# A recurrence with two MLPs behind it on one Trainium2 core: solve products added in place, gate and value as whole groups of eight matmuls, and a planner with numbered passes

## The chip, the cores and the metric

The kernel runs on one core of a Trainium2 chip. The metric is the time of one execution on the device in microseconds; the median of three runs is quoted, and one further execution was profiled.

## The reference, cut to what matters

```python
# batch 4, heads 8, 768 steps, head dimension 40
for t in range(S):                                   # attention-like recurrence
    y[:, :, t] = einsum('bhd,bhde->bhe', rt, state)
    Sa = einsum('bhde,bhe->bhd', state, at)
    state = state * wt[:, :, None, :] - einsum('bhd,bhe->bhde', Sa, bt) \
            + einsum('bhd,bhe->bhde', vt, kt)
x = y.transpose(0, 2, 1, 3).reshape(3072, 320)
h = x @ w_in                                         # 320 -> 2048
x = where(h >= 1, h, where(h <= -1, 0, (h + 1)**2 / 4)) @ w_out
g, val = x @ w_gate, x @ w_val                       # 320 -> 1536 each
out = (g / (1 + exp(-g)) * val) @ w_out2
```

All values are float32. The kernel keeps precision by splitting numbers into two float16 parts (high and low) and adding the products of the parts.

## The kernel before, in words

**Units.** The 768 steps are cut into 12 chunks of 64 steps (`c`); in each chunk there are four units, one for each batch (`j`), so 48 units `n = 4c + j`. Two units of a chunk share several loads and are called a pair (24 pairs, key `("mp", n // 2)`).

**The recurrence.** `p_tasks` prepares a unit's factors, `inv_tasks` inverts a chunk's triangular systems on VectorE (62 dependent small operations, lines L944 and L949, on the array `M`, 128 partitions by 16 by 32) and stores the result to DRAM (`tsd`, L969). `m_tasks` then does a unit's serial part. Its matmuls are, in order: `mm_x` (L1061), the solve product `mm_sa` for the first half of 32 steps (L1071, 8 matmuls, one for each head), `mm_c` (L1077), `mm_sa` for the second half, `mm_q` (L1138), `mm_y` (L1159). Between them ScalarE, VectorE and GpSimd split results into float16 parts (`xhi`, `xlo`, `xdup`, `shi`, `slo`). The stationary operand of `mm_sa` is a slice of the tile `tt`, which holds the inverse of both units of a pair; there is one `tt` buffer, so a pair's two loads (L1032: 64 partitions, L1036: 32 partitions) are issued after the last `mm_sa` of the pair before. `mm_sa` wrote its 32 rows of result to rows 64 to 127 of the PSUM tile `px`, from where `shi` and `slo` read them.

**The MLPs.** For a chunk of 256 tokens (all four batches), `in1` handles 256 hidden columns at a time: 16 matmuls of 128x256 (L1204, two groups of eight), then two ScalarE, one VectorE, one ScalarE and one GpSimd operation, then `outp` (L1293, 12 matmuls of 128x320, in two groups of six). There are 8 such pieces in a chunk. `in2` handles the gate and the value of 256 columns of the second MLP, 6 pieces in a chunk, each with its two PSUM tiles `ph`. The contraction over 320 needs, with the float16 parts, seven products over 128 rows and one over 64 rows. `in2_mm` does the seven (`full`, L1225) for gate and value, and the remaining 64-row products of gate and value in `half` (L1233): the gate's sit in rows 0 to 63 of the array, the value's in rows 64 to 127. Only when `half` is done may the gate's activation (L1276, ScalarE) and then the product with the value (L1279, VectorE) start.

**The order of the work.** All operations are entered as tasks with an engine, a cost, a priority and buffers. The class `Plan` simulates the engines (`forward`), then backward (`backward`) to get better priorities, repeats this, and emits the instructions of each engine in the order of a plan. So each engine's queue is fixed at build time, and TensorE waits in order for whatever stands next. A DMA's landing is assumed at `dma + 1.05`.

Of the kernel before, what the change touches and what calls it, by code (L numbers as in the profile page):

```python
# [15 lines left out]
class Plan:  # L16
# [28 lines left out]
    def task(self, eng, cost, emit, r=(), w=(), use=(), p=0.0, more=0.0, dma=0.0, slow=1.3, lk=False):  # L45
# [3 lines left out]
        for name, key in use:  # L49
# [3 lines left out]
            dma=dma, slow=slow, lk=lk or eng == "Pool", b=self.bias))  # L53
# [11 lines left out]
    def forward(self, prio):  # L65
# [59 lines left out]
        while done < len(ts):  # L125
            started = True
            while started:
                started = False
                for eng in self.ENGINES[:5]:
# [7 lines left out]
                    while any(heaps):  # L137
# [178 lines left out]
    def run(self):  # L316
# [3 lines left out]
        prio, best = [t["p"] + b for t, b in zip(self.tasks, bias)], None  # L320
        for _ in range(self.rounds):
            plan = self.forward(prio)
            if plan is None:
                break
            if best is None or plan[0] < best[0]:
                best = plan
            back = self.backward([-s - c for s, c in zip(plan[1], cost)])
            if back is None:
                break
            prio = [plan[0] - s - c + b for s, c, b in zip(back, cost, bias)]  # L330
# [8 lines left out]
def tile_recurrence__then__gated_mlps(  # L339
# [97 lines left out]
    sbt("tt", [128, 2, 2, H, HC], F16, 1)  # L437
# [102 lines left out]
    def TR(emit, dma, **kw):  # L540
        T("SP", 1.45, emit, dma=dma, **kw)
# [34 lines left out]
    def setup():  # L576
# [29 lines left out]
    def wpiece(names, key, src, n, m, dst_hi, dst_lo, scale, p, fit, r=(), also=None):  # L606
# [68 lines left out]
    def w_in_piece(name, src, dst, i, low, scale):  # L675
        if low:
            cs = slice(256 * i, 256 * i + 512)
            return ([(name, i), (name, i + 1)], (name, i, 2), src[1][i // 2].bitcast(I32), 64,
                    512, dst[0:64, 2, cs], dst[0:64, 2, cs] if name == "wv" else dst[64:128, 2, cs], scale)
# [234 lines left out]
    def inv_tasks(c, p):  # L914
# [38 lines left out]
        for i0 in range(0, 2 * HC - 2, span):  # L953
            part = [divmod(i, 2) for i in range(i0, min(i0 + span, 2 * HC - 2))]

            def steps(part=part):
# [4 lines left out]
              r=[(key, "j", i0)], w=[(key, "j", min(i0 + span, 2 * HC - 2))], use=ub + pm, p=p)  # L961
        T("ACT", c_s(512), lambda: s_.activation(
            out=T16()[:, 0], in_=M(), func=AF.Copy, scale=2.0**8),
          r=[(key, "j", 2 * HC - 2)], w=[(key, "h")], use=ub + pm, p=p)
        T("DVE", c_v(512), lambda: split(T16()[:, 1], M(), 2.0**8, T16()[:, 0]),
# [12 lines left out]
    def split_x(name, key, rows, src, scale, r, w, use, p, pool=False):  # L978
# [9 lines left out]
        def lo():  # L988
            t = x_tile(name, key)
            split(t[rows, 384:704], src(), scale, t[rows, 0:HD], e_)  # L990
            if name == "g":
                e_.tensor_copy(out=t[rows, 704:768], in_=t[rows, 640:704])
# [481 lines left out]
```

## Time and profile before

| | |
|---|---|
| median of three runs | 1107.91 us (1104.25 to 1110.54) |
| profiled execution | 1116.03 us, span 1113.9 us |
| busy TensorE / weight loads / VectorE / ScalarE / GpSimd | 900.9 / 712.6 / 772.2 / 720.0 / 714.1 us |
| granted TensorE clock, mean | 0.972 of full speed |

Busy time is the union of an engine's instructions. TensorE's matmuls are pipelined, so the distance from one matmul's start to the next tells more than the length that the profile shows of each. A share of the whole span hides that the first 400 us and the rest have different limits.

### The profile page before, as it was taken

Reading aid. Unit: us, or ns where it says so; the run is one execution under the profiler, and the core shown is the slowest. Engines: PE = TensorE matmul, PEld = TensorE weight load, DVE = VectorE, ACT = ScalarE, POOL = GpSimd, SP = SyncE. Lnnn points to the kernel's source line nnn. Section 1 sums busy time; section 2 is a strip of 40 time slices with the busy share of each in tenths; the row PEclk is TensorE's granted clock in tenths of the full one; section 3 lists DMA queues with packets and bytes.
Section 4 is the critical chain, followed back from the end, with each engine's and each line's share of the span. In section 5 each row is a group of like instructions: output and inputs, shape, how many; then the busy total and the mean of one; then the engine's idle time right before and its main releaser. Section 6 shows DMA issues by size and latency. Waiting matters only on the chain.

```text
span 1113.9 us, 28813 instructions
## 1 busy us (share of the span) xinstructions
PE 900.9 (81%) x10944; PEld 712.6 (64%) x10944; DVE 772.2 (69%) x1874; ACT 720.0 (65%) x1339; POOL 714.1 (64%) x980
## 2 busy tenths in 40 slices
PE   0321336757876999999999999999998999999998
PEld 0321225535654777877877787777786787787776
DVE  8688897997699577785876958768478477441210
ACT  1785576768776867768767777677686674644422
POOL 4588687756677778677785877758777464432222
PEclk9999999859898999999999999999999999999999
DMA  6976688688798689496794878857884444210000
GB/s 217 193 198 157 194 187 188 175 178 195 128 212 177 140 144 162 92 172 131 152 162 96 156 146 162 140 115 150 129 154 107 93 96 65 47 41 20 15 1 24
DMA packets 386195, 147.94 MB, mean 133 GB/s; under 512 B 344536, under 2 KB 362776, under 8 KB 386056
## 3 DMA queue, kind: packets, MB, share of 16 engines
q1 hardware_dynamic: 357735, 131.79, 57.4%
q10 hardware_dynamic: 28321, 14.31, 6.5%
q8 instruction: 85, 1.39, 0.6%
q14 instruction: 54, 0.44, 0.1%
HBM read 78.25 MB, written 21.52 MB: 90 GB/s over the span
## 4 chain that ended last, share of the span: by engine, by line
PE 34%; DVE 11%; DMA 7%; ACT 6%; issue 3%; POOL 1%; SPq 1%; POOLq 0%; ACTq 0%; DVEq 0%
PE po L1293 11%; PE ph L1225 9%; PE ph L1204 7%; DVE pg L949 2%; DVE ub L944 2%; DMA mx<-x 1%; PE pg L1159 1%; DMA vsT<-vss 1%; DMA tt<-tsd 1%; DVE vss L562 1%; PE ph L1233 1%; PE px L1071 1%; ACT ss L1168 1%; DMA ub<-lsd 1%; DVE mx L1279 1%
## 5 line engine op out<-in xcount | busy, mean ns | idle before, releaser
L1293 PE MATMUL po<-wo,mx 128*128 128x320 f16 x2016 | 320.2, 303 | 4.7 <-POOL mx L560 2.0
L560 POOL TENSOR_TENSOR mx<-mx 128x512 f16<-128x512 f32 x168 | 195.0, 1163 | 159.2 <-ACT mx L1250 146.2
L1293 PEld LDWEIGHTS <-mx 128*128 128x128 f16 x2016 | 187.9, 99 | 82.7 <-issue 14.7
L1204 PE MATMUL ph<-mx,w 128*128 128x256 f16 x1536 | 191.8, 278 | 12.8 <-DMA mx<-x 8.6
L1204 PEld LDWEIGHTS <-w 128*128 128x128 f16 x1536 | 149.6, 100 | 38.0 <-issue 9.7
L1225 PE MATMUL ph<-x2t,wg 128*128 128x256 f16 x1008 | 135.8, 275 | 7.0 <-ACT mx L1276 4.5
L1225 PE MATMUL ph<-x2t,wv 128*128 128x256 f16 x1008 | 135.0, 275 | 3.7 <-DVE mx L1279 1.7
L1250 ACT CAST mx<-mx 128x512 f16<-128x512 f32 x168 | 102.9, 615 | 42.0 <-DVE mx L1266 16.7
L1266 DVE SCALAR_TENSOR_TENSOR mx<-ph,mx 128x512 f32<-128x512 f32 x96 | 66.1, 689 | 77.4 <-ACT mx L1263 76.8
L1225 PEld LDWEIGHTS <-wg 128*128 128x128 f16 x1008 | 96.1, 98 | 23.1 <-issue 4.5
L1225 PEld LDWEIGHTS <-wv 128*128 128x128 f16 x1008 | 97.6, 98 | 17.8 <-issue 2.2
L1279 DVE SCALAR_TENSOR_TENSOR mx<-ph,mx 128x512 f32<-128x512 f32 x72 | 49.5, 687 | 83.7 <-ACT mx L1276 83.0
L944 DVE SCALAR_TENSOR_TENSOR ub<-ub,pg 128x126 f32<-128x126 f32 (+22 forms) x372 | 92.1, 248 | 21.0 <-DMA ub<-lsd 12.4
L949 DVE TENSOR_TENSOR pg<-pg,ub 128x126 f32<-128x126 f32 (+22 forms) x372 | 95.8, 257 | 8.2
L1276 ACT ACTIVATE mx<-ph 128x512 f32<-128x512 f32 x72 | 42.9, 596 | 78.0 <-PE ph L1233 69.9
L566 POOL TENSOR_TENSOR ldp<-ldp 64x320 f32<-64x320 f32 (+1 forms) x90 | 77.3, 869 | 5.1 <-DMA ldp<-was 1.1
L1262 ACT ACTIVATE mx<-ph 128x512 f32<-128x512 f32 x96 | 57.1, 594 | 25.0 <-PE ph L1204 21.6
L1102 ACT ACTIVATE vss<-px 32x640 f16<-32x640 f32 x90 | 62.0, 695 | 16.6 <-PE px L1071 14.1
L1093 POOL COPY xs<-xs 32x320 f16<-32x320 f16 x96 | 42.8, 449 | 31.1 <-ACT xs L1088 25.2
L1263 ACT ACTIVATE mx<-mx 128x512 f32<-128x512 f32 x96 | 60.5, 630 | 3.1
L884 DVE TENSOR_TENSOR pg<-pg,mask 64x512 f32<-64x512 f32 x48 | 33.1, 689 | 37.3 <-PE pg L881 19.4
L562 DVE SCALAR_TENSOR_TENSOR vss<-px,vss 32x320 f16<-32x320 f32 x90 | 44.3, 493 | 19.4 <-ACT vss L1102 16.6
(220 smaller groups left out, 1779.7 us busy)
## 6 DMA issues: line engine op xcount, KB each, us to landing
ub<-lsd SPq DMA_DIRECT2D x24, 256.0 KB
ldp<-in_kb_dram SPq DMA_DIRECT2D x18, 320.0 KB
ldv<-in_v_dram SPq DMA_DIRECT2D x18, 320.0 KB
wo<-in_wo_dram SPq DMA_DIRECT2D x15, 320.0 KB
ldp<-in_ar_dram SPq DMA_DIRECT2D x14, 320.0 KB
out_dram<-mx SPq DMA_DIRECT2D x23, 160.0 KB
ldp<-wks SPq DMA_DIRECT2D x20, 160.0 KB
wo<-in_w1a_dram SPq DMA_DIRECT2D x6, 512.0 KB
```

Source lines behind the costliest of these rows:

```text
L560: e.tensor_tensor(out=out, in0=x, in1=hi, op=ALU.subtract)
L566: e.tensor_tensor(out=out, in0=x, in1=y, op=ALU.mult)
L944: v_.scalar_tensor_tensor(out=t, in0=L()[:, j, j + 1:].unsqueeze(1).to_broadcast([128, nm, ni]), scalar=-(2.0**-10), in1=m[:, 0:nm, j:j + ...
L949: v_.tensor_tensor(out=m[:, 0:nm, j + 1:], in0=m[:, 0:nm, j + 1:], in1=t, op=ALU.add)
L1102: s_.activation(out=hi2(G("vss", key)[z]), in_=two(hd(G("px", key))[z]), func=AF.Copy, scale=2.0**-8)
L1204: t_.matmul(out=ps, lhsT=wts[:, wi, fs], rhs=xT[:, xi, :], start=(i == 0), stop=(i == len(plan) - 1))
L1225: t_.matmul(out=dst(a, f), lhsT=wts[:, wi, fs], rhs=G(*xk)[:, xi, :], start=(n == 0 and f == 0), stop=False)
L1250: T("ACT", c_s(512) - 0.04, lambda: s_.copy(out=G("g", key)[:, 0], in_=u2(key)), r=[(key, "u")], w=[(key, "gh")], use=U + GG, p=p)
L1263: s_.activation(out=u2(key), in_=u2(key), func=AF.Square, scale=2.0**3)
L1266: T("DVE", c_v(512, True), lambda: v_.scalar_tensor_tensor(out=u2(key), in0=ps2(key), scalar=2.0**8, in1=u2(key), op0=ALU.max, op1=ALU.min ...
L1279: T("DVE", c_v(512, True), lambda: v_.scalar_tensor_tensor(out=u2(key), in0=ps2(vk), scalar=2.0**-3, in1=u2(key), op0=ALU.mult, op1=ALU.mult),
L1293: t_.matmul(out=ps, lhsT=g[:, x, f, 128 * tt:128 * tt + 128], rhs=wo[:, 2 * i + f, y, :], start=(i == 0 and f == 0 and m == 0), stop=(i == ...
```

## The change

Four things are done. **(1)** `mm_sa` multiplies by a window of 128 columns of `tt` and adds into the rows of `px` that already hold its input (`start=False`), instead of writing 32 rows elsewhere. For this the inverse has its unit diagonal removed (`strict`, two small VectorE memsets a chunk) and its sign turned, `tt` gets a 64-column grid in which 32 columns are data and 32 are zero (one memset at the start), and its loads write runs of 32 numbers. `shi` and `slo` read the other rows of `px`. **(2)** `in2_mm` is gone: gate and value are each done as `in_mm` does it for the first MLP, two groups of eight matmuls over all 128 rows (the low part of the last 64 rows is padded with zeros, the extra ScalarE copy `also` of the value's weights is dropped), and the activation waits for the gate alone. **(3)** `outp` takes its first and last matmul by a count. **(4)** The planner makes 3 passes, keeps the priorities of the last pass that worked, adds offsets by kind, stage and step before and after the passes, and assumes landings at `dma + 1.705`; some lead times change.

```diff
-        self.bias = 0.0
-        self.lim, self.rounds, self.loose = 1.438, 14, ()
+        self.bias, self.unit, self.nudge, self.last = 0.0, ["z", 0, 0], ({}, {}), ({}, {})
+        self.lim, self.rounds, self.loose = 1.438, 3, ()
...
+    def offset(self, tables, t):
+        return tables[0].get(t["unit"][:2], 0.0) + tables[1].get(t["unit"][::2], 0.0)
...
-                            end = dma + 1.05
+                            end = dma + 1.705
...
+        best = self.forward([x + self.offset(self.last, t) for x, t in zip(good, self.tasks)])
...
-    sbt("tt", [128, 2, 2, H, HC], F16, 1)
+    tts = sbt("tt", [128, 8 * H * HC + HC], F16, 1)
...
+        v_.memset(tts[0], 0.0)
...
-        if also is not None:
-            T("ACT", c_s(m), lambda: s_.activation(
-                out=also, in_=u3(), func=AF.Copy, scale=scale), r=[(key, 3)], w=names, use=ux, p=p)
...
+        def strict():
+            for g in range(2):
+                v_.memset(G("pg", key)[64 * g:64 * g + 64, g:g + 15 * (HC + 2) + 1:HC + 2], 0.0)
+
+        T("DVE", 0.17, strict, r=[(key, "j", 2 * HC - 2)], w=[(key, "m")], use=ub + pm, p=p)
...
+            def tiles(a, b):
+                return G("tt", mp)[a:b, 0:8 * H * HC].rearrange("p (f b x) -> p f b x", f=2, x=C)[:, :, :, 0:HC]
+
             DMA(lambda e: e.dma_start(
-                out=G("tt", mp)[0:64].rearrange("p f j h t -> p f (j h t)"),
-                in_=td.rearrange("l s f b t -> (l s) f (b t)")),
+                out=tiles(0, 64), in_=td.rearrange("l s f b t -> (l s) f b t")),
                 r=[("tsd", c)], w=[(mp, "tt")], use=TT, p=p - 3, dma=0.5)
             DMA(lambda e: e.dma_start(
-                out=G("tt", mp)[64:96].rearrange("p f j h t -> p f (j h t)"),
-                in_=td[0].rearrange("s f b t -> s f (b t)")),
+                out=tiles(64, 96), in_=td[0]),
                 r=[("tsd", c)], w=[(mp, "tt")], use=TT, p=p - 3, dma=0.25, cost=0.68)
...
         def mm_sa(hf):
-            sa, tt, xs = hd(G("px", key)), G("tt", mp)[0:96, hf, j % 2], G("xs", (key, hf))[0:96]
-            z = 64 + 32 * hf
+            sa, tt, xs = hd(G("px", key)), G("tt", mp)[0:96], G("xs", (key, hf))[0:96]
             for h in range(H):
-                t_.matmul(out=sa[z:z + 32, h], lhsT=tt[:, h], rhs=xs[:, h])
+                o = C * (2 * H * hf + H * (j % 2) + h) - HC * hf
+                t_.matmul(out=sa[:, h], lhsT=tt[:, o:o + 128], rhs=xs[:, h], start=False, stop=(h == H - 1),
+                          skip_group_check=True)
...
-    def in2_mm(key, vk, i, xk, p):
...
-        in2_mm(key, vk, i, ("x2t", c), p)
+        in_mm(key, wg, "wg", ("x2t", c), i, p, [("x2t", c)], (key, "h"))
+        in_mm(vk, wv, "wv", ("x2t", c), i, p, [("x2t", c)], (vk, "h"))
...
-          r=[(key, "t")], w=[(key, "u")], use=U + [("ph", vk)], p=p)
+          r=[(key, "t"), (vk, "h")], w=[(key, "u")], use=U + [("ph", vk)], p=p)
...
+    by_chunk = by({
+        "a": {1: 3.58, 3: 1.46, 6: 0.68, 10: -1.14},
...
```

**Order, first place: gate and value on TensorE.** The rows are one of the last pieces of the second MLP, before the change; `ph_131` and `ph_132` are the gate's and the value's PSUM tiles, and only the first rows of each run of equal kind are shown.

```order
L1225 LDWEIGHTS wg
L1225 MATMUL ph_131<-x2t_123,wg 128x256
...
L1225 LDWEIGHTS wv
L1225 MATMUL ph_132<-x2t_123,wv 128x256
...
L1293 MATMUL po_133<-wo_67,mx 128x320
...
L1233 LDWEIGHTS wg
L1233 MATMUL ph_131<-x2t_123,wg 128x256
L1233 LDWEIGHTS wv
L1233 MATMUL ph_132<-x2t_123,wv 128x256
...
L1293 MATMUL po_134<-wo_67,mx 128x320
```

Before, the runs were seven gate, seven value, seven gate, seven value, six of `outp`, and then the four half-height matmuls that end the group. With the change the same piece reads:

```order
L1217 LDWEIGHTS wg
L1217 MATMUL ph_131<-x2t_123,wg 128x256
...
L1217 LDWEIGHTS wv
L1217 MATMUL ph_132<-x2t_123,wv 128x256
...
L1284 MATMUL po_133<-wo_67,mx 128x320
...
L1284 MATMUL po_134<-wo_67,mx 128x320
```

Now 16 of the gate stand first, then 16 of the value, and nothing behind `outp` belongs to the piece any more.

**Order, second place: TensorE between two pairs.** The rows stand between the last `mm_sa` of units 28 and 29 and the first of unit 30 (chunk 7), one row of each run; the runs are 8 matmuls long, those of L1293 six, and `tt` is loaded anew in this stretch. Before:

```order
L1071 MATMUL px_128<-xs_116,tt_118 32x40
...
L1204 MATMUL ph_131<-mx,w_63 128x256
...
L1138 MATMUL pg_129<-art_81,vsT_100 128x64
...
L1061 MATMUL px_127<-vss_96,lsp 128x40
...
L1204 MATMUL ph_131<-mx,w_63 128x256
...
L1293 MATMUL po_134<-wo_66,mx 128x320
...
L1071 MATMUL px_127<-xs_117,tt_118 32x40
```

In full there were two runs of L1204, one of L1138, three of L1061 and three of L1293. With the change (L1083 is `mm_sa`, L1217 `in_mm`, L1284 `outp`, L1073 `mm_x`):

```order
L1083 MATMUL px_128<-xs_116,tt_118 128x40
...
L1217 MATMUL ph_132<-x2t_123,wv 128x256
...
L1284 MATMUL po_133<-wo_66,mx 128x320
...
L1073 MATMUL px_127<-vss_96,lkt_88 128x40
...
L1284 MATMUL po_134<-wo_66,mx 128x320
...
L1217 MATMUL ph_131<-mx,w_63 128x256
...
L1083 MATMUL px_127<-xs_117,tt_118 128x40
```

In full there are now four runs of eight of L1217, three of L1073 and two of six of L1284.

**Order, third place: VectorE at the end of the first chunk's inverse.** L944 and L949 are the inverse's last steps, L635, L639 and L645 unpack weights, L732 to L788 belong to the decay factors, and L562 with `ub` is the split that precedes the store of the inverse. Before:

```order
L639 SCALAR_TENSOR_TENSOR px_128<-wv,px_128 128x512
L944 SCALAR_TENSOR_TENSOR ub_124<-ub_124,pg_130 128x70
...
L949 TENSOR_TENSOR pg_130<-pg_130,ub_124 128x16
L905 TENSOR_TENSOR lkt_88<-pg_129,lkt_88 64x512
L562 SCALAR_TENSOR_TENSOR ub_124<-pg_130,ub_124 128x512
L645 SCALAR_TENSOR_TENSOR wo_67<-wv,px_128 128x512
```

With the change:

```order
L954 TENSOR_TENSOR pg_129<-pg_129,ub_124 128x16
L653 SCALAR_TENSOR_TENSOR wo_67<-wo_67,px_128 128x320
L969 MEMSET pg_129 64x16 x2
L643 TENSOR_SCALAR px_128<-wo_67 128x320
L751 COPY wg<-wv 128x40
L756 COPY wg<-wv 32x40 x4
L647 SCALAR_TENSOR_TENSOR px_128<-wo_67,px_128 128x320
L569 SCALAR_TENSOR_TENSOR ub_124<-pg_129,ub_124 128x512
```

The split stood at row 179 of VectorE's queue and stands at row 171 now; the memsets are new, and instead of one operation seven stand between the inverse's last step and the split (the memsets counted as one row).

## Rows read from the trace of the kernel before

**Rows 1.** The page: busy tenths in 40 slices of 27.8 us.

```profile
PE   0321336757876999999999999999998999999998
```

**Rows 2.** Windows by stage: width, busy us (and count) of each engine, TensorE clock, DMA share, GB/s.

```profile
174.00:400.00 226.00, 169.60 (x2025) 129.30 (x2024) 180.39 (x410) 164.62 (x310) 160.98 (x210) 0.87 0.82 173
400.00:700.00 300.00, 289.50 (x3755) 232.60 (x3753) 228.98 (x562) 219.08 (x416) 226.12 (x283) 1.00 0.77 144
```

**Rows 3.** Waits of TensorE from 400 us on: us in total, times, longest.

```profile
PE px L1071 <- DMA tt<-tsd: 3.4, 4, 1.5
PE ph L1225 <- ACT mx L1276: 2.9, 5, 0.7
...
PE ph L1225 <- DVE mx L1279: 1.6, 4, 0.6
```

**Rows 4.** Timeline of TensorE's matmuls around a solve product: start, length, tile, shape.

```profile
603.86 1.04 PE L1204 MATMUL ph<-mx,w 128*128 128x256 f16 x8
604.83 0.37 PE L1071 MATMUL px<-xs,tt 96*32 96x40 f16 x8
605.13 1.80 PE L1293 MATMUL po<-wo,mx 128*128 128x320 f16 x12
...
608.52 0.56 PE L1077 MATMUL px<-vss,l 128*128 128x40 f16 x16
608.92 0.75 PE L1159 MATMUL pg<-kbs,wt 128*128 128x40 f16 x24
```

**Rows 5.** Windows of L1071 alone: TensorE and weight-load busy us and counts.

```profile
400.00:1000.00 600.00, 23.16 (x520) 16.76 (x520) 1.00 0.66 124
```

**Rows 6.** Windows of L1233 alone, same columns.

```profile
400.00:1114.00 714.00, 25.47 (x260) 7.40 (x260) 1.00 0.56 106
```

**Rows 7.** Timeline of TensorE's matmuls in two late pieces of the second MLP.

```profile
1075.01 0.99 PE L1293 MATMUL po<-wo,mx 128*128 128x320 f16 x6
1075.84 0.93 PE L1225 MATMUL ph<-x2t,wg 128*128 128x256 f16 x7
...
1078.90 0.98 PE L1293 MATMUL po<-wo,mx 128*128 128x320 f16 x6
1079.81 0.28 PE L1233 MATMUL ph<-x2t,wg 64*128 64x256 f16 x1
...
1080.13 0.99 PE L1293 MATMUL po<-wo,mx 128*128 128x320 f16 x6
...
1085.24 0.92 PE L1225 MATMUL ph<-x2t,wg 128*128 128x256 f16 x7 [0.74 <-ACT mx L1276]
```

**Rows 8.** Timeline of the last piece: the activation that waits for L1233.

```profile
1105.78 0.60 ACT L1276 ACTIVATE mx<-ph 128x512 f32<-128x512 f32 x1 [3.96 <-PE ph L1233]
```

**Rows 9.** Windows around one store of an inverse, one load of `tt`, one of decays.

```profile
942.00:946.00 4.00, 4.00 (x38) 3.13 (x35) 0.55 (x1) 0.62 (x1) 1.16 (x1) 1.00 0.65 85
948.00:950.00 2.00, 2.00 (x21) 1.80 (x19) 0.00 (x0) 0.49 (x2) 1.16 (x1) 1.00 0.34 98
935.00:937.00 2.00, 2.00 (x20) 1.80 (x19) 1.87 (x5) 1.32 (x2) 1.03 (x2) 1.00 0.62 117
```

**Rows 10.** Timeline of SyncE's queue: issues of those transfers.

```profile
934.11 0.63 SPq L1022 DMA_DIRECT2D waf<-was  x1
...
942.09 1.63 SPq L969 DMA_DIRECT2D tsd<-ub  x2
946.91 0.54 SPq L1032 DMA_DIRECT2D tt<-tsd  x1
```

**Rows 11.** Timeline between the first and second pair of chunk 4.

```profile
457.57 0.54 SPq L1032 DMA_DIRECT2D tt<-tsd  x1
...
462.39 0.27 PE L1071 MATMUL px<-xs,tt 96*32 96x40 f16 x4
```

**Rows 12.** VectorE's timeline: the idle time before the first decay data.

```profile
3.19 0.48 DVE L602 MEMSET ss<- 64x512 uint32 x1
...
5.91 6.21 DVE L566 TENSOR_TENSOR wg<-wg 128x80 f32<-128x80 f32 x16 [1.79 <-DMA wg<-in_w_dram]
```

More of the change, by code (lines that the diff above doesn't have):

```diff
@@ L319, in run @@
         bias = [t["b"] for t in self.tasks]
-        prio, best = [t["p"] + b for t, b in zip(self.tasks, bias)], None
-        for _ in range(self.rounds):
+        bias = [b + self.offset(self.nudge, t) for t, b in zip(self.tasks, bias)]
+        prio, good = [t["p"] + b for t, b in zip(self.tasks, bias)], None
+        for n in range(self.rounds):
             plan = self.forward(prio)
             if plan is None:
[L324 to L330, printed above, removed]
+                if good is None:
+                    break
+                prio = [(x + y) / 2 for x, y in zip(prio, good)]
+                continue
+            good = prio
+            if n < self.rounds - 1:
+                back = self.backward([-s - c for s, c in zip(plan[1], cost)])
+                prio = [plan[0] - s - c + b for s, c, b in zip(back, cost, bias)]
+        best = self.forward([x + self.offset(self.last, t) for x, t in zip(good, self.tasks)])
         end, _, order, self.slots = best
@@ L540, in TR @@
     def TR(emit, dma, **kw):
[L541 removed]
+        T("SP", 1.381, emit, dma=dma, **kw)
     def hd(ap):
@@ L991, in lo @@
             if name == "g":
-                e_.tensor_copy(out=t[rows, 704:768], in_=t[rows, 640:704])
+                e_.memset(t[rows, 704:768], 0.0)
         T(eng, cost + (0.2 if name == "g" else 0.0), lo, r=[(w, 0)], w=[w], use=use + X, p=p)
@@ L1096, in xlo @@
             xs = G("xs", (key, hf))
-            split(xs[64:96], hd(G("px", key))[32 * hf:32 * hf + 32], -(2.0**-10),
+            split(xs[64:96], hd(G("px", key))[32 * hf:32 * hf + 32], -(2.0**-8),
                   xs[0:32])
@@ L1101, in shi @@
             z = slice(64 + 32 * hf, 96 + 32 * hf)
-            s_.activation(out=hi2(G("vss", key)[z]), in_=two(hd(G("px", key))[z]),
-                          func=AF.Copy, scale=2.0**-8)
+            s_.activation(out=hi2(G("vss", key)[z]), in_=two(hd(G("px", key))[32 * hf:32 * hf + 32]),
+                          func=AF.Copy, scale=-(2.0**-10))
         def slo(hf):
@@ L1294, in mm @@
                         out=ps, lhsT=g[:, x, f, 128 * tt:128 * tt + 128],
-                        rhs=wo[:, 2 * i + f, y, :], start=(i == 0 and f == 0 and m == 0),
-                        stop=(i == nl and f == 1 and m == 2))
+                        rhs=wo[:, 2 * i + f, y, :], start=(n == 1 and f == 0 and m == 0),
+                        stop=(n == nl + 1 and f == 1 and m == 2))
         for tt in range(2):
@@ new lines, in by @@
+    def by(tables):
+        return {(u, i): x for u, table in tables.items() for i, x in table.items()}
+    by_chunk = by({
+        "i": {11: 2.04},
+        "m": {0: -0.7},
+        "p": {3: 0.64},
+    })
+    by_step = by({
+        "b": {11: -1.09},
+        "d": {32: -0.71, 35: -1.8, 58: 1.33, 69: 5.43, 78: -0.84},
+        "i": {58: 0.34},
+    })
+    K.nudge = by_chunk, by_step
+    by_chunk = by({
+        "a": {1: 3.58, 3: 1.46, 6: 0.68, 10: -1.14},
+        "b": {1: 6.03, 7: 1.56, 8: -1.13},
+        "i": {0: 2.2, 4: 0.19, 7: -4.3, 11: -3.15},
+        "m": {9: -0.42, 14: 2.48, 18: -1.71, 20: 1.2, 23: 1.58, 25: 1.41, 26: 1.55, 29: -0.2, 33: -0.67,
+            37: 1.43, 43: -0.05, 47: 2.74},
+        "p": {3: 0.02, 4: 0.08, 8: -2.64, 10: 1.86, 13: 2.29, 16: -1.68, 21: -3.2, 22: -1.99, 23: -1.48,
+            24: 0.88, 25: 5.14, 27: -1.33, 30: 0.44, 31: -9.83, 36: -2.57, 37: -0.21, 41: 1.8, 42:
+            0.85},
+        "v": {0: 0.49, 3: -3.84, 5: 0.13, 8: -7.5, 10: -3.71, 13: 3.68, 14: -4.2, 15: 0.29, 16: 1.33},
+        "w": {0: 10.05, 4: -1.95},
+    })
@@ L1367, in tile_recurrence__then__gated_mlps @@
                 fit = ("late", "high") + (("low",) if i < NLO else ())
-                also = dst[64:128, 2, 256 * i:256 * i + 512] if l and nm == "wv" else None
-                x = wpiece(*w_in_piece(nm, src, dst, i, l, 2.0**6), p=LPRI + LSTEP * len(late), fit=fit, r=free,
-                           also=also)
+                x = wpiece(*w_in_piece(nm, src, dst, i, l, 2.0**6), p=LPRI + LSTEP * len(late), fit=fit, r=free)
                 late.append(x)
@@ L1399, in pad0 @@
         p_.memset(ss0[64:128], 0.0)
-    K.bias = 0.0
+    K.bias, K.unit = 0.0, ["z", 0, 0]
     T("Pool", 1.3, pad0, r=[(x, n) for n in range(B) for x in ("lk", "l2")] + [("lsd", 0)], w=["pad0"], p=-200.0)
@@ L1417, in tile_recurrence__then__gated_mlps @@
     for x in pend:
+        K.unit = ["o", 0, 0]
         outp(*x, t)
```

66 lines of the change are left out of this document (27 added, 39 removed), and 13 rows, old and new, of the table by_step.

## The prediction

> **What bounds the kernel now.** I first read the page's slices of TensorE [rows 1]. In the first thirteen of 40 slices the digits lie between 0 and 8; from the fourteenth on (362 us) nearly all are 9; I cut at 400 us, where the windows are clean. So two stages have different limits. The windows by stage say the same in time [rows 2]: from 174 to 400 us TensorE is busy 169.6 of 226 us, at a granted clock of 0.87 of full speed, and VectorE is busier (180.4); from 400 to 700 us TensorE is busy 289.5 of 300 us at full clock, VectorE 229.0, the DMA engines 0.77. Behind 400 us the end is therefore set by how long TensorE's queue takes to run through; before it, by VectorE, the DMAs and the serial recurrence. A microsecond taken from TensorE's queue counts in full in the second stage and little in the first.
>
> What is left of waiting in the second stage is small. The list of waits [rows 3] gives 3.4 us in four waits for the load of `tt`, 2.9 in five for the gate's activation and 1.6 in four for the product with the value, which free the two `ph` tiles. The change touches just these.
>
> **The change part by part.** The sum is made against the profiled execution, 1116.03 us (span 1113.9). That run is 8.1 us above the median of the three, 1107.91; I carry the result over by ratio.
>
> *Solve products.* A run of eight 128x256 matmuls takes a quarter of 32, which the late pieces show in 3.06 us for 28 (1075.84 to 1078.90, [rows 7]), so 0.109 each and 0.87 for eight. In [rows 4] eight of that shape start at 603.86 and the solve product starts at 604.83, 0.97 later: 0.10 is lost on entering it. It then holds the queue for 0.30 us (604.83 to 605.13). L1077, with the same 40 columns on the moving side but 128 weight columns, holds it 0.40 us for sixteen (608.52 to 608.92), half of them with 96 rows, so 0.20 for eight. The profile marks the one 96\*32 and the other 128\*128: the loss stands where the array's tile shape changes. With 128 columns and 96 rows the new product has the shape of L1077's second half, and I price it as that: 0.20 in place of 0.40 us, less 0.01 for reading, 0.19 saved. From 400 us on there are 520 such matmuls [rows 5], 65 groups: **-12.4 us** (-11 to -13). In the first 400 us 31 groups lie in a stage that waits for others; each still stands in a serial chain, at most 31 x 0.19 = 5.9, at least 0. I take **-1.5**.
>
> *Gate and value.* In the late piece [rows 7] six of `outp` take 0.83 us when L1225 follows (1075.01 to 1075.84), but 0.91 when the half-height matmuls follow (1078.90 to 1079.81): 0.08 lost on entering. The four then take 0.32 (to 1080.13): 0.40 in all. Four full ones take 4 x 0.109 = 0.44. For the 260 behind 400 us [rows 6], 65 groups: **+2.6 us**; with the 0.02 or 0.03 by which single starts are read wrong, +1 to +4.
>
> The Trainium skill, TensorEngine Tiling (Array Packing), section Performance Considerations, says that a contraction of 64 or less may be tiled by rows so that two products run at once, up to 2 times as fast. That speaks against this part. By it the four cost 0.22 and the change adds 65 x 0.22 = 14 us where the row gives 2.6. The same page, under Key Properties, says that a change of tiling mode drains the engine; both rows above agree with that, 0.08 and 0.10 on entering.
>
> *Waits for the tiles.* The gate's activation could start only behind the half-height matmuls, which came after the value; at 1085.24 the next gate waited 0.74 us for it [rows 7]. Now it can start behind sixteen matmuls, while sixteen of the value (1.75 us) still run, and it takes 0.60 [rows 8]; the tile is free before the next group asks. The value's tile is freed by VectorE, within about 1 us of the value's end, while the next gate's 1.75 run. Of 2.9 + 1.6 us I take **-4.0** back (0 to -4.5). Three fewer `also` copies and the count in `outp` change nothing on TensorE. At the end the last activation, 0.60 us, is no longer in the chain: **-0.6**.
>
> *Loads of `tt`.* They wrote 192 runs of 1 KB a pair; now 64 x 32 + 32 x 32 = 3072 runs of 64 bytes. No row of before shows such a load. The nearest is the store of an inverse, 4096 runs of 64 bytes: issued at 942.09 [rows 10], it keeps 16 engines busy 0.65 of 4 us, 2.6 us [rows 9]; 3072 would take 1.96. The load of decays reads 1024 runs of 160 bytes and takes at most 0.62 x 2 = 1.25 us; 3072 would take 3.75. The old load took 0.34 x 2 = 0.68. So each pair's load takes 1.3 to 3.1 us longer. The rows with 64 bytes are the nearest, and I go by 1.3.
>
> The Trainium skill, DMA: Bandwidth & Descriptors, section Specifications, puts the least size for full rate at 512 bytes and 27 GiB/s for an engine. If a run of 64 cost as much as one of 512, an estimate from that page would be 3072 x 17.7 ns / 16 = 3.4 us, near the upper bound. The row with 64 bytes does not agree, but it is a store.
>
> Is there cover? The load of 946.91 was done by 950, 3.1 us behind its first issue. In chunk 4 the second pair's load is issued at 457.57 and its first product starts at 462.39, 4.8 us later, with no wait [rows 11]. So 1.3 longer fits and 3.1 does not, by 1.4. The order of the changed kernel leaves slightly more there: before unit 30, 5.0 us of matmuls before and, counted likewise, 5.7 now (four runs of eight at 0.87, two of six at 0.83, three of `mm_x` at 0.20 like L1077). The first pair of a chunk waits behind the inverse's store and has no such cover except what the planner puts there: it now assumes each landing 0.655 us later, twice in that chain, 1.3 us. For 16 pairs behind 400 us: 0 to 16 x 1.6 = 25 us. I take **+2**. What stands behind the waiting product in TensorE's queue is MLP work, so the whole engine stops with it.
>
> *The rest.* Two memsets a chunk lie on VectorE and in the inverse's chain; a memset of 512 words a row took 0.48 us [rows 12] and these write 16, so at most 1 us a chunk, under TensorE's cover behind 400 us. The memset of `tt` has 1040 words a row; 512 words took 0.48 [rows 12], so about 1 us, and VectorE sits idle 1.79 us there, waiting for the first decays. If that cover is gone it costs its 1 us. The new order in the first 400 us moves the first inverse's split up by eight rows and puts weight work between its last step and the split. Against each other I call these **0**, with -10 to +8: TensorE idles 56 us between 174 and 400, and the first stage's end can move either way.
>
> Sum: -12.4 - 1.5 + 2.6 - 4.0 - 0.6 + 2 = -13.9. The profiled execution would be 1102.1 us, a ratio of 0.9875, and the median **1094 us**.
>
> **The rivals.**
>
> *Late `tt`* (slower). If the short runs land later than the cover reaches, TensorE stops at the first solve product of every pair. Without the +2 the other terms give -15.9; to eat them up takes 16 x 1.0 us behind 400 us, and to end more than 0.5% slower 16 x 1.35. At 1.6 us each it is 1107.91 - 15.9 + 25.6 = 1117.6 us. For it: four waits of `tt` already stand in rows 3, so some loads have no slack. Against it: the 64-byte store's 1.3 and the later landing that the planner assumes. With half of that, the result is within 0.5%.
>
> *The first stage ends earlier.* TensorE idles 56 us from 174 to 400 us. If the order brings a quarter of that, 14 us, the time is 1080. For it: VectorE and the DMAs have gaps too (180.4 of 226, 0.82). Against it: the same recurrence and the same weights go through VectorE, with more instructions.
>
> *Row tiling pays.* If the half-height pairs are in truth worth 0.22 us a group as the Tiling page would have it, the term is +14 and not +2.6, and the time is 1105 us. The measured 0.32 and 0.08 speak against it.
>
> *Nothing is gained from the solve product.* If adding in place costs what the change of shape did, 12.4 us stay and the time is 1106. Against it: L1077 also adds into `px` with 96 rows, at 0.20 us for eight.
>
> **How the numbers follow.** My forecast, with its own range of 1085 to 1102 us, has 0.62. The first stage shorter: 0.13. Late `tt`: 0.17, of which 0.10 ends slower and 0.07 within 0.5%. Row tiling or no gain from the solve product: 0.08, within 0.5%. Half a per cent (5.5 us) is about what a measurement of this kernel can tell from no change. So faster (below 1102.4) 0.75, same 0.15, slower 0.10. The range that leaves out no more than 2 in 10 reaches from 1077 to 1108.
>
> **What the changed kernel's profile would show.** The solve product would be marked 96\*128 and eight would hold TensorE's queue 0.20 us with no loss before them; sixteen gate matmuls and then sixteen of the value in 3.5 us, and no 64\*128 rows. TensorE's waits for L1276 and L1279 would be nearly gone, those for `tt` at most a few us; if that row grows to 15 us or more, the late load is the cause of whatever is missing. TensorE's busy time from 400 us to the end would still be near 97%. Wrong would be a first stage that ends 10 us earlier or later, seen in where the slices turn to 9.

## The result and the profile after

The changed kernel took 1094.05 us, the median of four runs (1090.31 to 1098.03), beside 1106.95 for the kernel before: a ratio of 0.9873, with a 95% interval of 0.9841 to 0.9905. The forecast was 1094. In a second set of runs the same kernel gave 1092.67 beside 1109.09, 0.9845 (0.9807 to 0.9883). So the number was right, but by luck: the runs below show that two errors of opposite sign cancelled in it.

The profiled execution took 1091.0 us (span 1089.3). TensorE's slices on its page, against [rows 1]:

```profile
PE   0331335657985999999999999999999999999998
PEclk9999999867996999999999999999999999999999
```

Windows by stage, in the columns of [rows 2]:

```profile
174.00:400.00 226.00, 174.43 (x2217) 139.06 (x2217) 190.64 (x451) 171.17 (x325) 169.49 (x219) 0.87 0.90 183
400.00:700.00 300.00, 288.17 (x3720) 241.39 (x3717) 221.62 (x555) 217.80 (x414) 217.78 (x274) 1.00 0.80 140
```

From 174 to 400 us TensorE now gets through 2217 matmuls in place of 2025: the program is further on at 400 us. The prediction had named a first stage that ends 10 us earlier or later as the sign that it was wrong, and that sign is here: the 2,800th matmul starts at 398.3 us in place of 410.4. In the slices it hardly shows.

TensorE's waits from 400 us on, as in [rows 3] (L1083 is the solve product now, L1217 the one product of all three MLP matrices):

```profile
PE px L1083 <- DMA tt<-tsd: 6.1, 6, 2.0
PE ph L1217 <- ACT mx L1264: 2.2, 2, 2.0
```

The waits for the `ph` tiles went from 4.5 us (gate's activation and product with the value) to 2.2, and those for `tt` rose from 3.4 to 6.1, by 2.7, near the +2 of the forecast. Around a solve product TensorE's timeline now reads (start, length, tile, shape):

```profile
599.99 1.04 PE L1217 MATMUL ph<-x2t,wg 128*128 128x256 f16 x8
600.87 0.36 PE L1083 MATMUL px<-xs,tt 96*128 96x40 f16 x8
601.08 1.03 PE L1217 MATMUL ph<-x2t,wg 128*128 128x256 f16 x8
```

From 599.99 to 600.87 is 0.88 us for eight products of the MLP, and from 600.87 to 601.08 the solve product holds the queue for 0.21: next to no loss on entering, as forecast, where [rows 4] had 0.97 and 0.30. The late pieces run without a gap; from the gate to the next gate, 1041.55 to 1046.67, are 5.12 us:

```profile
1041.55 1.91 PE L1217 MATMUL ph<-x2t,wg 128*128 128x256 f16 x16
1043.29 1.91 PE L1217 MATMUL ph<-x2t,wv 128*128 128x256 f16 x16
1045.04 1.79 PE L1284 MATMUL po<-wo,mx 128*128 128x320 f16 x12
1046.67 1.91 PE L1217 MATMUL ph<-x2t,wg 128*128 128x256 f16 x16
```

Apart from the first stage, this looks like the forecast come true. It is a trap: each row shows what an operation does where it stands, and none shows what the time would have been without it. For that each part was undone alone, or done alone.

### The profile page after: what moved, and what is told of

Read it like the earlier page. It is cut to its first block, busy times and chain, and to the rows that moved or that the text cites. A ratio compares the mean times of both kernels' runs of the same rounds, so it can differ in the third digit from the quotient of the medians.

```text
span 1089.3 us, 28798 instructions
## 1 busy us (share of the span) xinstructions
PE 882.7 (81%) x10944; PEld 730.8 (67%) x10944; DVE 763.4 (70%) x1899; ACT 716.8 (66%) x1336; POOL 711.5 (65%) x980
## 4 chain that ended last, share of the span: by engine, by line
PE 40%; DVE 22%; DMA 12%; ACT 9%; issue 5%; POOL 3%; SPq 2%; ACTq 0%; POOLq 0%; DVEq 0%
PE ph L1217 21%; PE po L1284 14%; DMA mx<-x 4%; DVE ub L949 3%; DVE pg L954 3%; DVE vss L569 2%; DMA tt<-tsd 2%; DMA ub<-lsd 2%; PE pg L1172 1%; DVE px L643 1%; DVE px L647 1%; DMA vsT<-vss 1%; ACT ss L1181 1%; DVE xs L569 1%; PE px L1083 1%
## 5 line engine op out<-in xcount | busy, mean ns | idle before, releaser
L1284 PE MATMUL po<-wo,mx 128*128 128x320 f16 x2016 | 309.1, 300 | 2.6 <-POOL mx L567 1.8
L1284 PEld LDWEIGHTS <-mx 128*128 128x128 f16 x2016 | 190.6, 98 | 70.0 <-POOL mx L567 3.4
L1217 PE MATMUL ph<-mx,w 128*128 128x256 f16 x1536 | 196.1, 282 | 25.0 <-DMA mx<-x 19.4
L1217 PEld LDWEIGHTS <-w 128*128 128x128 f16 x1536 | 151.2, 101 | 51.8 <-issue 17.9
L1217 PE MATMUL ph<-x2t,wg 128*128 128x256 f16 x1152 | 142.8, 272 | 2.3 <-ACT mx L1264 2.2
L1217 PE MATMUL ph<-x2t,wv 128*128 128x256 f16 x1152 | 141.3, 273 | 0.0
L1217 PEld LDWEIGHTS <-wg 128*128 128x128 f16 x1152 | 108.6, 97 | 16.9 <-issue 2.9
L1217 PEld LDWEIGHTS <-wv 128*128 128x128 f16 x1152 | 109.9, 98 | 13.0
L949 DVE SCALAR_TENSOR_TENSOR ub<-ub,pg 128x126 f32<-128x126 f32 (+22 forms) x372 | 91.8, 247 | 14.3 <-DMA ub<-lsd 4.2
L1115 ACT ACTIVATE vss<-px 32x640 f16<-32x640 f32 x90 | 60.8, 689 | 20.2 <-PE px L1083 15.7
L1083 PEld LDWEIGHTS <-tt 96*128 96x128 f16 x768 | 29.7, 98 | 39.1 <-issue 18.1
L1191 POOL COPY gf<-ss 40x960 f16<-40x960 f16 x41 | 40.3, 984 | 19.1 <-DVE ss L569 9.3
```

Source lines behind the costliest of these rows:

```text
L949: v_.scalar_tensor_tensor(out=t, in0=L()[:, j, j + 1:].unsqueeze(1).to_broadcast([128, nm, ni]), scalar=-(2.0**-10), in1=m[:, 0:nm, j:j + ...
L1115: s_.activation(out=hi2(G("vss", key)[z]), in_=two(hd(G("px", key))[32 * hf:32 * hf + 32]), func=AF.Copy, scale=-(2.0**-10))
L1217: t_.matmul(out=ps, lhsT=wts[:, wi, fs], rhs=xT[:, xi, :], start=(i == 0), stop=(i == len(plan) - 1))
L1284: t_.matmul(out=ps, lhsT=g[:, x, f, 128 * tt:128 * tt + 128], rhs=wo[:, 2 * i + f, y, :], start=(n == 1 and f == 0 and m == 0), stop=(n == ...
```

## The experiments

Most runs keep an order fixed: some take the changed kernel and undo something, three ("in the order of before") take the kernel before and do one thing. Where nothing else is said, every engine executes the same list in the same order as the kernel it was made from. Single executions of one kernel differ by up to 17 us, so times are medians of 6 to 12 runs, each with the ratio to the kernel before on the same chip; an interval of a ratio is plus or minus 0.2 to 0.4%, 2 to 4 us. In the edits, `...` stands for lines left out.

**The changed kernel again.** No edit.

> The changed kernel again, beside the three edits of it on the same chip: 0.987 of the kernel before, 1092 to 1096 us, by any theory.

Measured: 1092.67 us, as said above. The edits of the changed kernel are compared with this time.

**The solve product's columns, undone.**

```diff
-                o = C * (2 * H * hf + H * (j % 2) + h) - HC * hf
-                t_.matmul(out=sa[:, h], lhsT=tt[:, o:o + 128], rhs=xs[:, h], start=False, stop=(h == H - 1),
+                o = C * (2 * H * hf + H * (j % 2) + h)
+                z = HC * hf
+                t_.matmul(out=sa[z:z + 32, h], lhsT=tt[:, o:o + 32], rhs=xs[:, h], start=False, stop=(h == H - 1),
```

> The changed kernel in its own order, with one thing undone: the solve product takes 32 columns of the weights again (still added in place), so the array's tile is 96*32. Theory of the tile shape: eight hold TensorE's queue 0.30 us with 0.10 lost ahead of them in place of 0.20 with none, so 65 groups behind 400 us give back 12.4 us and the first stage up to 1.5: 1106 to 1108 us, 0.999 to 1.002 of the kernel before. Rival, the new order brings the gain: it stays at 0.987, 1094 us. Half of each: 1100 us.

Measured: 1101.92 us, 0.9928 (0.9900 to 0.9955), 9.3 us longer than the changed kernel. Its timeline at the same place in the program:

```profile
611.60 1.04 PE L1218 MATMUL ph<-x2t,wg 128*128 128x256 f16 x8
612.56 0.37 PE L1084 MATMUL px<-xs,tt 96*32 96x40 f16 x8
612.87 1.05 PE L1218 MATMUL ph<-x2t,wg 128*128 128x256 f16 x8
```

Eight products of the MLP take 0.96 before the 96\*32 tile, and the solve product 0.31, in place of 0.88 and 0.21: the loss of 0.18 comes with the tile's shape, with everything else equal. In time it is worth 9 us here, two thirds of the 13.9 forecast: between the two theories, nearer to the first.

**Gate and value as before.**

```diff
...
+            if a and f:
+                for g in range(2):
+                    for b, wts in enumerate((wg, wv)):
+                        z = slice(64 * b, 64 * b + 64)
+                        t_.matmul(out=dst(b, g), lhsT=wts[z, 2, fs], rhs=G(*xk)[z, 5, :], start=False, stop=(g == 1))
...
```

(`a` and `f` count the matrix and its half; the four stand behind the value's second seven.)

> The changed kernel in nearly its own order, with the gate and the value as before: seven matmuls each, then four of half height for both, and the gate's activation behind them (the low part of the value's last rows is read in place of the high one, so the output is not the reference's; the work is the same). Theory: TensorE's work falls by 65 x 0.02 to 0.04 us = 1.3 to 2.6, the waits for the gate's activation and the product with the value come back with about 4 and the end with 0.6: 1095 to 1098 us, 0.989 to 0.992 of the kernel before. Rival, whole groups bring more through the order than their waits: 1100 us or more. Rival, half heights side by side pay: 14 us less, 1080 us.

Measured: 1108.38 us, 0.9989 (0.9959 to 1.0018), 15.7 us longer, far above what I expected. It does not price the grouping: to keep the two tiles from blocking each other the planner had to pull the value's products forward, and about one row in six of ScalarE's list stands elsewhere. Among its longest waits from 400 us on are those for the inputs of the first MLP and for that MLP's product on VectorE, neither of which the edit touches:

```profile
PE ph L1227 <- DMA mx<-x: 8.5, 4, 3.8
...
PE ph L1227 <- DVE mx L1263: 5.9, 7, 2.8
```

It is inconclusive on the grouping, and a first sign of what a slightly other order costs.

**Loads of `tt` in long runs.** The solve product still takes 128 columns, of a packed tile.

```diff
-                return G("tt", mp)[a:b, 0:8 * H * HC].rearrange("p (f b x) -> p f b x", f=2, x=C)[:, :, :, 0:HC]
+                return G("tt", mp)[a:b, 0:8 * H * HC].rearrange("p (f y) -> p f y", f=2)[:, :, 0:2 * H * HC]
...
-                out=tiles(0, 64), in_=td.rearrange("l s f b t -> (l s) f b t")),
+                out=tiles(0, 64), in_=td.rearrange("l s f b t -> (l s) f (b t)")),
...
```

> The changed kernel in its own order, with the loads of tt in runs of 1 KB as before and packed, 192 a pair in place of 3072 of 64 bytes (the solve product then reads other columns than it should, so the output is not the reference's; the matmuls are the same). Theory: the load takes 1.4 us less of the engines and lands about 1.5 us earlier, the waits for tt behind 400 us go from 6.1 to about 3.4 us: 1090 to 1093 us, 0.984 to 0.987. Rival, the short runs cost more, by holding up other transfers in the first stage: 1088 us or less. Rival, the load is covered and costs nothing: 1094 us.

Measured: 1076.56 us, 0.9699 (0.9662 to 0.9736): 16.1 us shorter than the changed kernel, where the theory said 1 to 4. The rival of a costly load is right in its size; that it acts by holding up other transfers in the first stage is not shown.

**Short runs alone, in the order of before.**

```diff
-    sbt("tt", [128, 2, 2, H, HC], F16, 1)
+    sbt("tt", [128, 2, 2, H, C], F16, 1)
...
-                out=G("tt", mp)[0:64].rearrange("p f j h t -> p f (j h t)"),
-                in_=td.rearrange("l s f b t -> (l s) f (b t)")),
+                out=G("tt", mp)[0:64].rearrange("p f j h t -> p f (j h) t")[:, :, :, 0:HC],
+                in_=td.rearrange("l s f b t -> (l s) f b t")),
...
-                t_.matmul(out=sa[z:z + 32, h], lhsT=tt[:, h], rhs=xs[:, h])
+                t_.matmul(out=sa[z:z + 32, h], lhsT=tt[:, h, 0:HC], rhs=xs[:, h])
```

> The kernel before in its own order, with one thing of the change: tt lies on a grid of 64 columns, so each pair's load is 3072 runs of 64 bytes in place of 192 of 1 KB; the solve product still reads 32 columns. The prediction's term: +2 us, 1.002 of the kernel before. By the run that undid it in the changed kernel, which was 16 us shorter: +10 to +20, 1.010 to 1.018, and then the short runs are the cost, not how the new order meets them.

Measured: 1125.92 us beside 1109.42, 1.0148 (1.0115 to 1.0181): 16.5 us. In the changed order the same runs cost 16.1 us with 128 columns (the run above) and 12.8 with 32 (1101.92 us against the 1089.09 of the order alone, below). The waits for `tt` from 400 us on grew by 3.6 us only:

```profile
PE px L1071 <- DMA tt<-tsd: 7.0, 5, 2.1
```

Over the whole run they grew by 9.7 us; before, and with short runs:

```profile
  DMA tt<-tsd: 22.9, 7
  DMA tt<-tsd: 32.6, 10
```

**128 columns alone, in the order of before.**

```diff
...
-                t_.matmul(out=sa[z:z + 32, h], lhsT=tt[:, h], rhs=xs[:, h])
+                o = HC * (2 * H * hf + H * (j % 2) + h)
+                t_.matmul(out=sa[:, h], lhsT=tt[:, o:o + 128], rhs=xs[:, h], start=False, stop=(h == H - 1),
...
```

> The kernel before in its own order, with one thing of the change: the solve product takes 128 columns and adds in place, while tt stays packed in 1 KB runs (the columns read are then not those of the block alone, so the output is not the reference's; the work is the same). The prediction's term: -12.4 - 1.5 = -13.9 us, 0.987 of the kernel before. By the run with 32 columns in the changed kernel: -9, 0.992. Rival, the queue's gain is eaten by later waits: 0.995 or more.

Measured: 1107.73 us, 0.9983 (0.9962 to 1.0004): 1.7 us, no change that can be measured. TensorE's busy time did fall, from 900.9 us on the page of before to

```profile
PE 883.0 (80%) x10944; PEld 710.0 (65%) x10944; DVE 770.5 (70%) x1875; ACT 719.2 (65%) x1339; POOL 712.4 (65%) x980
```

that is 17.9 us for 96 groups, 0.19 each. Part of this may be the clock (the mean granted clock was 0.972 before and 0.978 here): two pairs of pages in the changed order, where it was nearly equal, give 10.5 and 13.4 us. The rival is right in this order: TensorE did less, and the time hardly changed. The profiled execution was the shortest of the twelve, 1101.93 us, so its span compares badly. A stretch without the first stage compares better, from the first solve product of the fifth chunk to the last solve product of all, in the columns of [rows 2]; before, and with 128 columns:

```profile
450.50:990.70 540.20, 520.98 (x6695) 416.45 (x6695) 386.60 (x922) 376.79 (x710) 359.53 (x449) 1.00 0.65 122
439.90:977.00 537.10, 511.93 (x6697) 416.47 (x6696) 384.69 (x922) 376.52 (x710) 358.82 (x449) 1.00 0.66 123
```

TensorE worked 9.0 us less there and stood idle 6.0 more (25.2 in place of 19.2), so 3.1 were left. Such differences are rough: two executions of the changed kernel took 532.9 and 527.4 us for this stretch.

**Whole groups alone, in the order of before.**

```diff
-            for n, (xi, wi) in enumerate(((0, 0), (0, 3), (1, 1), (1, 4), (2, 2), (3, 0), (4, 1))):
+            for n, (xi, wi) in enumerate(((0, 0), (0, 3), (1, 1), (1, 4), (2, 2), (3, 0), (4, 1), (5, 2))):
...
         def half():
...
+            pass
```

> The kernel before in its own order, with one thing of the change: gate and value as whole groups of eight, no half-height products, so the gate's activation waits for the gate alone (the low part is multiplied with both halves of the weights' last rows, so the output is not the reference's; the work is that of the changed kernel). The prediction's terms: +2.6 - 4.0 - 0.6 = -2 us, 0.998. By the run that put the half heights back, 15.7 us longer: -10 or more, 0.991 or less, if that was the grouping and not its new order. Rival, row tiling pays: +14, 1.013.

Measured: 1109.75 us, 1.0004 (0.9976 to 1.0032). The forecast of -2 and no change both lie in the interval (-2.7 to +3.6 us); -10 and +14 do not, nor does the +9.4 that the three terms make with the rival's 14 in place of 2.6. TensorE's busy time is 900.8 us beside 900.9.

**Zeros stored with the inverse.**

```diff
-        tsd[c] = dr.tile([2, HC, 2, BH, HC], F16, name=f"tsd{c}")
+        tsd[c] = dr.tile([2, HC, 2, BH, C], F16, name=f"tsd{c}")
...
+            v_.memset(L()[:, :, HC // 2:], 0.0)
...
-                in_=T16()[64 * g:64 * g + 64].rearrange("p l m t -> p (l m) t")),
+                in_=TP()[64 * g:64 * g + 64].rearrange("p l m t -> p (l m) t")),
...
```

> The changed kernel in its own order, with the same values in tt, but the grid's zeros are stored with the inverse: the store writes 4096 runs of 128 bytes in place of 64, each pair's load reads 192 runs of 2 KB in place of 3072 of 64 bytes, and one memset of 512 words a chunk (about 0.5 us on VectorE) zeroes the gaps. If short runs are what costs 16 us, and a run of 128 bytes costs hardly more than one of 64: 1077 to 1081 us, 0.970 to 0.974 of the kernel before. Rival, the store's doubled bytes or the load's doubled bytes cost as much: 1085 to 1095 us.

Measured: 1096.79 us, 0.9893 (0.9857 to 0.9930): nothing gained, 1.8 us above even the rival's range. By the packet records a run of 2 KB takes 121 ns, and a pair's load lands 4.0 us behind its first issue, 0.5 before the 4.5 of the short runs; and the store's 4096 runs take 13.4 ns each with 128 bytes, about 10.1 with 64, so it holds 16 engines 3.4 us in place of 2.6. In the two stores of this run beside which no other 128-byte packets ran, the last packet landed 5.3 us behind the first issue; the same two took 3.8 in the changed kernel. What the store, the load and the additional memset cost apart was not measured.

**The order alone.** The changed kernel's order, with 32 columns and packed loads.

```diff
...
-                t_.matmul(out=sa[:, h], lhsT=tt[:, o:o + 128], rhs=xs[:, h], start=False, stop=(h == H - 1),
+                o = HC * (2 * H * hf + H * (j % 2) + h)
+                t_.matmul(out=sa[HC * hf:HC * hf + HC, h], lhsT=tt[:, o:o + HC], rhs=xs[:, h], start=False, stop=(h == H - 1),
...
```

> The changed kernel's order with the solve product of before: 32 columns (added in place, at the rows it solves) and tt packed, loaded in 1 KB runs; gate and value stay whole groups, which in the order of before were worth nothing. What is left of the change is then in the main its order. If the prediction's term for the order (0) holds: 1107 us, 0.998 of the kernel before. If the runs so far add up (1092.7 + 9.3 - 16.1): 1086 us, 0.979, and the order alone brings 23 us.

Measured: 1089.09 us, 0.9802 (0.9764 to 0.9840): 20.1 us shorter than before, with the old width of the solve product and the old loads. What this run has besides the order is the whole groups of gate and value, the adding in place, two memsets a chunk and three copies fewer; none of these but the groups was run apart.

**A mixed solve product.** The half that may overwrite the other rows takes 128 columns, the other half 32, from a packed tile.

```diff
...
+                o = HC * (2 * H * hf + H * (j % 2) + h - hf)
+                m = 128 if hf else HC
+                t_.matmul(out=sa[0:m, h], lhsT=tt[:, o:o + m], rhs=xs[:, h], start=False, stop=(h == H - 1),
...
```

> The changed kernel's order with tt packed and loaded in 1 KB runs, the second half's solve product with 128 columns in place, the first half's with 32 (the 128 of a packed tile would change rows that the second half still needs). By the runs so far: 1092.7 - 16.1 + half of 9.3 = 1081 us, 0.974. If the long runs gained only because other columns were read: 1092 or more. If a change of the array's tile costs nothing: 1077.

Measured: 1078.72 us, 0.9721 (0.9688 to 0.9755). It computes all of the reference and beats both kernels: 30 us under the one before, 14 under the changed one.

**The planner of before, with all of the changed work.**

```diff
-        self.lim, self.rounds, self.loose = 1.438, 3, ()
+        self.lim, self.rounds, self.loose = 1.438, 14, ()
...
-                            end = dma + 1.705
+                            end = dma + 1.05
...
```

The old passes and parameters are in the lines left out, and the tables of offsets are unused.

> All work of the changed kernel (matmuls, loads, memsets) under the planner of before: its passes, landings, parameters, no tables of offsets. If the order is worth nothing, as the prediction had it: 1094 us, 0.987. If the terms measured in the order of before add up (1109.4 + 16.5 - 1.7 + 0.4): 1125 us, 1.014.

Measured: 1115.32 us, 1.0043 (1.0014 to 1.0073). Without its order the change makes the kernel 6 us slower, not faster. It is 9 us better than the sum of the parts; that this planner could lay out its own order around the cheaper product may be why, and was not tried apart.

**Two tiles of `tt`.** As the mixed product, with a pool of two.

```diff
-    tts = sbt("tt", [128, 4 * H * HC + 2 * HC], F16, 1)
+    tts = sbt("tt", [128, 4 * H * HC + 2 * HC], F16, 2)
...
```

> As the run with half of the solve products at 128 columns and 1 KB runs, but with two tiles of tt, so that a pair's load need not wait until the pair before has read its own; the planner lays the order out anew, with offsets that were not made for it. If the load between two pairs on the one tile is what makes short runs costly, the long one costs some of it still: below 1081 us, about 1075. If the order's offsets are worth more than that: above 1090.

Measured: 1109.86 us, 0.9999 (0.9977 to 1.0022). The new plan threw away 31 us, more than the order had brought. What a second tile is worth in a given order stays open.

## Why the forecast came out, and what was wrong in it

| step | forecast, us | in the order of before | in the changed order |
|---|---|---|---|
| 128 columns in place | -13.9 | -1.7 | -9.3 (short runs), -12.5 (long runs) |
| gate and value, three terms | -2.0 | +0.3 | not separated |
| loads of `tt` | +2 | +16.5 | +16.1 (128 columns), +12.8 (32 columns) |
| the order, with whole groups | 0 | | -20.1 |

The last column is from 1109.1 to 1089.1 for the order, to 1076.6 for the columns with long runs, to 1092.7 with short ones, the changed kernel itself; these three add up to the changed kernel's -16.4 by construction, so their sum shows nothing new. Of the forecast's terms the columns were near (12.5 measured, with long runs). The loads cost 14 us more than forecast, the order and the groups together brought 18 more, and these two errors nearly cancelled.

*The loads of `tt`* were the first step that failed. I priced the lateness rightly: by the packet records a pair's last packet lands 3.2 us (median of 24) behind the first issue in the kernel before, 4.5 in the changed one, 3.2 again with long runs, so 1.3 later. What failed was the cover. I read it at one pair. The first solve product of a pair starts within 0.7 us of the landing in 5 of 24 pairs before, in 11 of 24 after the change, in 5 again with long runs. The rival of the late `tt`, at 0.17, is what happened in part, at 13 to 16 us of its 25. In the changed order the delay shows behind the first stage: from the fifth chunk's first solve product to the last one, with long runs and in the changed kernel:

```profile
437.10:959.30 522.20, 512.75 (x6760) 431.17 (x6759) 380.38 (x938) 376.00 (x713) 357.07 (x449) 1.00 0.67 126
437.70:970.60 532.90, 514.94 (x6760) 431.85 (x6759) 381.63 (x938) 376.64 (x713) 357.03 (x449) 1.00 0.69 123
```

Of the 10.7 us more, 8.5 are TensorE's idle time (5.2 and 5.0 in the other execution of the changed kernel). In the order of before the kernel with short runs starts its 2,800th matmul at 416.8 us in place of 410.4, the last one at 1124.4 in place of 1110.3, so a part seems to arise in the first stage; but the two other kernels in that order, with long runs, start the 2,800th at 400.8 and 407.5, so single executions don't settle it.

*The order* was the second, called 0 with -10 to +8. With the whole groups it brought 20 us, more than the rival of a shorter first stage had (14), and not in the first stage alone: the fourth chunk's first solve product starts at 362.8 us in place of 371.9, 9 us earlier, and the rest of the gain comes behind it. In single executions this point spreads from 363.5 to 378.8 in the four kernels with the order of before and from 355.2 to 366.2 in seven with the changed order, so its size is known only roughly. From the fifth chunk's first solve product to the last one the order alone takes

```profile
441.10:974.50 533.40, 521.09 (x6758) 431.94 (x6758) 380.82 (x938) 376.15 (x713) 356.22 (x450) 1.00 0.66 123
```

in place of 540.20 us: TensorE worked as long (521.09, 520.98) and stood idle 12.3 us in place of 19.2. The rows of the solve product show the end (how many; shortest, median and longest in ns; first and last start in us; the shapes counted in every fourth). Before:

```profile
L1071 PE MATMUL px<-xs,tt x720: 179/179/216, 132.3 to 990.5; 96*32 96x40 f16 x180
```

The order alone:

```profile
L1083 PE MATMUL px<-xs,tt x712: 179/179/216, 126.7 to 974.3; 96*32 96x40 f16 x178
```

The span was 1113.9 us in the first and 1093.3 in the second, so the last solve product started 16.2 us earlier and what follows took 119.0 in place of 123.4. The same row of others, with the span and what is left of it behind the last solve product. Short runs alone, 1128.1, 123.8 left:

```profile
L1071 PE MATMUL px<-xs,tt x720: 179/179/217, 133.9 to 1004.3; 96*32 96x40 f16 x180
```

128 columns alone, 1100.2, 123.3 left:

```profile
L1072 PE MATMUL px<-xs,tt x720: 179/180/216, 132.0 to 976.9; 96*128 96x40 f16 x180
```

Whole groups alone, 1108.5, 121.3 left:

```profile
L1071 PE MATMUL px<-xs,tt x720: 179/179/216, 132.4 to 987.2; 96*32 96x40 f16 x180
```

The changed kernel, 1089.3, 118.9 left:

```profile
L1083 PE MATMUL px<-xs,tt x712: 178/180/216, 128.5 to 970.4; 96*128 96x40 f16 x178
```

The mixed product, 1073.9, 118.9 left:

```profile
L1084 PE MATMUL px<-xs,tt x712: 179/179/215, 126.6 to 955.0; 96*32 96x40 f16 x90, 96*128 96x40 f16 x88
```

Zeros stored, 1103.1, 118.9 left:

```profile
L1086 PE MATMUL px<-xs,tt x712: 179/180/241, 131.9 to 984.2; 96*128 96x40 f16 x178
```

32 columns with short runs, 1103.7, 119.0 left:

```profile
L1084 PE MATMUL px<-xs,tt x712: 178/180/216, 129.2 to 984.7; 96*32 96x40 f16 x178
```

Within one order the rest is the same to half a microsecond, unless the late pieces themselves are edited, while the span moves by 30 us: the difference had arisen by the last solve product, and behind it stands a fixed rest of MLP work. This alone doesn't tell what bounds the part before it: TensorE's list is fixed and nearly full, so a late product keeps its distance from the end whether the recurrence or TensorE's own work delayed it. These are single executions (the one of before was 7 to 9 us above its medians, that of 128 columns alone 6 under), which moves a span, but not the fixed rest.

*What bounds the kernel.* "A microsecond taken from TensorE's queue counts in full" behind 400 us held in one order and not in the other. In the order of before, the stretch shown with the 128 columns gave back 3.1 of 9.0 us. In the changed order (order alone, then long runs with 128 columns) TensorE worked 8.3 us less in the same stretch, and it was 11.2 shorter. The stretches are single executions; the medians say the same, with 1.7 us against 9.3 and 12.5. TensorE was 97% busy before the change, as I read it now, because the planner fills its queue with MLP pieces up to the moment at which the next product of the recurrence should be ready; this reading is argued, not shown. Which waits took the gain in the order of before was not isolated.

*The solve product* was priced well: the timeline loses 0.18 us a group at 96\*32, for the 0.19 of the forecast, and in the changed order 9 to 13 us reach the end. *Gate and value*: the sum of -2 is compatible with +0.3; whole groups alone shortened the rest behind the last solve product by 2.1 us (121.3 from 123.4), of the sign and size of the -2 though it did not show in the median, and under the planner of before with all of the changed work it was 121.5 as well. That row tiling pays 14 us is excluded, by the time and by TensorE's equal busy time; what whole groups bring in the changed order stays open. *The last activation* has no run of its own.

On the rules of the Trainium skill: that a change of tiling mode drains the engine (TensorEngine Tiling (Array Packing), Key Properties) agrees with 0.18 us lost a group at 96\*32 and next to none at 96\*128. The Trainium skill's factor of up to 2 for row tiles (the same page, Theoretical Speedup) did not show in a stream of full tiles: TensorE's busy time was 900.9 us with the half-height products and 900.8 without. The estimate from the Trainium skill's DMA: Bandwidth & Descriptors, Specifications, 3.4 us for a pair's short runs, is above what the load measured, 3072 x 10.8 ns / 16 = 2.1 us.

## What to carry to other kernels

When an order is planned so that one engine fills every gap, its busy share does not say what work taken from it is worth: the same cut of the solve product was worth 2 us in one order and 9 to 13 in another. Compare, between two fixed points of the queue, how its busy and its idle time change. A late landmark (here the last solve product) tells in other runs on which side of it a difference arose, not what caused it. A load that feeds a serial chain is not priced by its cover at one link: here it was 1.3 us later at 24 links, which would be 31 us; counted only where no slack is left, at 11 of them, it is 14 as an estimate, and 13 to 16 were measured. And an edit that comes with a new plan should be measured under both plans: here the plan, with the whole groups, brought 20 us, and the loads that the edit made longer gave 13 to 16 of them back.

## What the hardware showed unexpectedly

A run of 64 bytes read from DRAM took 10.8 ns on its DMA engine, one of 1 KB 57 to 68 (over six runs), one of 2 KB 121 (means over the packets of `tt`, beside the other transfers of each kernel): sixteen times the bytes for five to six times the time, and from 1 to 2 KB about in proportion. A store's run took about 10.1 ns with 64 bytes (9.4 in the kernel before) and 13.4 with 128. So for a tile of 64-byte pieces neither short runs (2.1 us of 16 engines) nor padding them (1.5) comes near the packed load (0.7).
